# Attention scores on TensorE: three 64-row products in the two row halves instead of two 128-row products, operands split in place, TensorE's order fixed by hand

## The chip, the core and the metric

The kernel runs on one core of a Trainium2 chip. A core has TensorE for matrix products, VectorE, ScalarE and GpSimd for elementwise work, and SyncE, which issues most of the DMA transfers; 16 DMA engines carry them. Each engine works through its own list of instructions in order, and semaphores hold an instruction back until what it needs is there. The metric is the time of the whole kernel on the device in microseconds. Three runs of the kernel before took 747.27, 748.15 and 751.06 us; the median is 748.15.

## What is computed

The reference is attention with a bias that depends on the positions, followed by a two-layer feed-forward part ("MoE" in the names). Four batches, eight heads, 576 positions, head width 64; the feed-forward part has 2304 tokens, 512 inputs and 2048 hidden columns.

```python
scores = scale * np.matmul(q, k.transpose(0, 1, 3, 2))
x = (psi_rel / psi_i)[..., None]
h = np.maximum(x @ w1 + b1, 0.0)
bias = h @ w2
scores = scores + bias.transpose(2, 0, 1)[None, :, :, :]
attn = np.exp(scores - np.max(scores, axis=-1, keepdims=True))
attn = attn / (np.sum(attn, axis=-1, keepdims=True) + 1e-09)
return np.matmul(attn, v).astype(np.float32)
...
h = x @ w_in
g = np.where(pos, h, np.where(neg, 0.0, (h + beta) ** 2 / (4.0 * beta)))
return (g @ w_out).astype(np.float32)
```

All inputs are float32. Products run on TensorE in its rounded form of float32 (fp32r). To keep the accuracy the kernel parts an operand in two: a high part, which is the operand rounded, and a low part, which is what the rounding left out. A product of two operands is then high x high + high x low + low x high.

## The kernel before

The program has three stages, one after the other: the position bias (until 69.84 us in the profile), attention, and the MoE products.

Attention takes the heads in pairs: NP = 4 pairs times B = 4 batches make N = 16 passes n. In a pass the 576 queries of each of the two heads j are cut in four blocks k of 128 rows; the last 64 rows of both heads share a fifth, narrow block "L". A score row has 576 columns and is made in two halves hf of HS = 288, which lie in two banks of PSUM. The pool psS holds two such tiles S, four banks.

**Scores** (`scores`, L441). For each head and half two products of 128 rows add up in PSUM. The first multiplies the queries and, below them in rows 64 to 127, the low part of the queries by the high keys, which lie twice, in rows 0 to 63 and again in rows 64 to 127 (`qs`, `kh`; L455). The second multiplies the queries, with zeros below, by the low keys (`q0`, `kl`; L456). The fifth block has four products per half (L476, L477). VectorE takes S out of PSUM, adds the bias and finds the row's extreme (L458, L478; called the eviction below: tile e, extreme mx); ScalarE makes the exponential in place and sums it (L465, L484).

**Transposes and values.** TensorE transposes e in pieces of 128 x 128 (tiles T, L521; T_L for the narrow block, T_s for what two blocks share). T is parted in hi and lo: ScalarE and VectorE do it (L496, L497), or, for the tiles in POOL, ScalarE copies T to c (L501) and VectorE or GpSimd make hi (L503, L505) and GpSimd lo (L506). The value products O then run over hi and lo in two halves of the queries (L559, L561), ScalarE copies them to x, and R transposes the row sums (L545).

**Preparing a pass** (`prep`, L149). SyncE loads keys and queries in one tile qk (keys in rows 0 to 63, queries in rows 64 to 127, 1216 columns) and the values; GpSimd's queue loads the queries a second time, broadcast into both halves of qa (L167). VectorE casts qk to its high part kh (L163), GpSimd subtracts and gets the low part ls in two pieces (L136). Then two transfers per piece move data between partition halves: the low queries from ls into qa (L199) and the high keys from kh's upper to its lower half (L200). `step` and the table t say in which half step of which earlier pass each of these is issued.

**The order** is made by the program in the order of the calls. A queue holds the transposes and values of earlier blocks; `drain` issues them when the queue is longer than dr[k]. TensorE's instructions are not pinned: the framework's scheduler may move them, and does so.

Beside the passes, attention carries work for the next stage (called guests in the prediction): weights of the first MoE columns (WQ) and its inputs (XQ).

Of the kernel before, what the change touches and what calls it, by code (L numbers as in the profile page):

```python
# [21 lines left out]
P = 128  # L22
# [5 lines left out]
QW = 1216  # L28
# [3 lines left out]
CFG = dict(un=[('paaa', 'paav')[g in (1, 30, 32, 34)] for g in range(NG)], ex=(9, 2, 0, 2, 9), bb=5, mv=1, hi='pvvpv', rb='a', lag=(1, 1), dr=(3, 1, 2, 2, 2), pool=((0, 1), (2, 0), (2, 1), (3, 0), (3, 1)), sb=4, keep=1, drain=2, diag='a', rb2='v', eps='v', rc=2, rbb=1, hb=2, rawb=(2, 2), t=(3, 10, 11, 10, 18, 11, 12, 19), eb=4, seq=0, pb=(6, 9, 12, 14, 16), pq=22, tb=6, ub=12, low0='ppp', anch=(8, 8, 16, 23, 23), low1='ppp', ob=4, gb=4, fin=2, lastp=15, xs=2, sbf=('v', 'v', 'v', 'v', 'v'), bsE=(), ytail='p')  # L32
# [3 lines left out]
FIRST = ((0, 3), (1, 4), (2, 5), (3, 33))  # L36
# [11 lines left out]
def attn_cpb_moe_kernel(ctx, tc, qk, vL, cb, win, wout, lw, ident, ii, out):  # L48
# [26 lines left out]

    qa = [ac.tile([P, 2, QW], F32R, name=f"qa{i}") for i in range(2)]
    last_y, stored, copied, narrow = [], [], {}, []
# [71 lines left out]
    def prep(n):  # L149
# [10 lines left out]
        def high_k():  # L160

            a["k"] = qp.tile([P, QW], F32R, tag="kh", name=f"kh{n}", bufs=CFG["hb"])
            high(nc.vector.tensor_copy(a["k"], a["r"]))  # L163

        def load_q():
            a["q"] = qa[n % 2]
            (keep if n == 1 else pool)(nc.gpsimd.dma_start(out=a["q"][:D], in_=qk[n, D:P].unsqueeze(1).to_broadcast((D, 2, QW))))  # L167

        def load_r():
            a["r"] = lp.tile([P, QW], F32, tag="qk", name=f"qk{n}", bufs=CFG["rawb"][0])  # L170
# [16 lines left out]
        def part(i):  # L187


            def f():  # L190
                if i == 0:
                    a["l"] = qp.tile([P, QW], F32R, tag="kl", name=f"ls{n}")
# [3 lines left out]
                with ExitStack() as after:  # L196
                    if n == 1:
                        after.enter_context(tc.issue_after(stored[-1].ins))
                    nc.sync.dma_start(out=a["q"][D:P, 0, c].bitcast(F32), in_=ls[D:P, c].bitcast(F32))  # L199
                    copied[n] = nc.sync.dma_start(out=kh[D:P, c].bitcast(F32), in_=kh[:D, c].bitcast(F32))  # L200
                if (n, i) == (1, 1):
                    with tc.issue_after(copied[1].ins):
# [7 lines left out]
        return [load_r, load_q, load_v, high_k, high_v, part(0), part(1), v_]  # L210
# [4 lines left out]
    with ExitStack() as ph:  # L215
# [24 lines left out]
        for t in qa:  # L240
            nc.gpsimd.memset(t[D:P, 1, :].bitcast(F32), 0.0)

# [84 lines left out]
        for G in range(NG):  # L327
# [3 lines left out]
            if G == 0:  # L331
                for i in range(3):
                    preps[0][i]()
            for i, g_ in zip((3, 5, 6, 4, 7), CFG["pb"]):
# [22 lines left out]
    def x_tile(z, k, part, name):  # L357
# [4 lines left out]
        if at % 3 == 0 or at == 7:  # L362
            tag, w, n_ = ("qk", QW, CFG["rawb"][0]) if g < 2 else ("v", 10 * D, CFG["rawb"][1])
# [53 lines left out]
    with ExitStack() as ph:  # L417
# [22 lines left out]

        def scores(n, k, qkv, bias):  # L441
            qs, q0, kh, kl = qkv["q"][:, 0], qkv["q"][:, 1], qkv["k"], qkv["l"]
# [5 lines left out]
            if k < 4:  # L448
                e = ep.tile([P, 2 * S], F32, tag="e", name=f"e{n}_{k}")
                for j in range(2):  # L450
                    ps = psS.tile([P, 2, 512], F32, tag="S", name=f"S{n}_{k}_{j}")
                    qc = slice(P * k, P * k + P) if j == 0 else slice(704 + P * k, 704 + P * k + P)
                    for hf in range(2):
# [652 lines left out]
```

## Time and profile before

| | |
|---|---|
| median of three runs | 748.15 us |
| runs | 747.27 to 751.06 us |
| span of the profiled execution | 749.8 us |
| TensorE busy with products | 703.8 us (94%) |
| VectorE, ScalarE, GpSimd busy | 537.5, 518.8, 519.1 us |
| bytes moved by DMA | 103.37 MB |

The profile is of one execution of the kernel; its span runs from the first to the last instruction. It is not one of the three timed runs, and the page states no other time for it. A busy product on TensorE contains the time until its result is out, and the next one starts before that; how densely TensorE works is therefore read from the starts of neighbouring products and not from their durations. A wait is put down to the engine that ended it. DMA share is the mean busy share of the 16 DMA engines.

### The profile page before, as it was taken

To read this page: it belongs to the slowest core of one execution; us is meant where nothing else is said; L and a number is where in the kernel's file an instruction comes from. 1 tells how busy PE (TensorE), PEld (TensorE's weight loads), DVE (VectorE), ACT (ScalarE), POOL (GpSimd) and SP (SyncE) were. 2 spreads that over 40 slices of the span, in tenths; PEclk is the share of its full clock that TensorE was granted. 3 is DMA by queue.
4 is the path that set the end of the run, shared out by engine and by line. 5 is a ranking of instruction groups with operands and counts; after the bars stand their busy time and mean duration, and the time that the engine had idled before them with its cause. 6 is when DMAs were issued, how large, how long until landed. Compare 5 with 4: busy or idle time off the path is not lost.

```text
span 749.8 us, 13722 instructions
## 1 busy us (share of the span) xinstructions
PE 703.8 (94%) x4640; PEld 621.8 (83%) x4640; DVE 537.5 (72%) x1043; ACT 518.8 (69%) x1156; POOL 519.1 (69%) x440
## 2 busy tenths in 40 slices
PE   4687999899999999989999999999999999999997
PEld 1234999888888898989988898989899988888886
DVE  7899888868898888886877776354455465666653
ACT  8896989869888998986656565344444547666563
POOL 9887778858878888871757677565656545665662
PEclk9899999989999999999999999999999999999999
DMA  8887799996997797744364645023021002000002
GB/s 228 231 271 228 200 249 240 238 234 167 233 275 192 186 271 190 177 121 162 95 199 135 197 147 163 35 83 90 7 63 32 1 1 84 1 1 1 0 1 85
DMA packets 58662, 103.37 MB, mean 138 GB/s; under 512 B 12496, under 2 KB 32736, under 8 KB 58592
## 3 DMA queue, kind: packets, MB, share of 16 engines
q1 hardware_dynamic: 56000, 92.31, 43.5%
q0 software_dynamic: 2304, 9.96, 6.4%
q8 instruction: 37, 0.61, 0.3%
q14 instruction: 33, 0.27, 0.1%
q10 hardware_dynamic: 288, 0.22, 0.1%
HBM read 67.38 MB, written 25.12 MB: 123 GB/s over the span
## 4 chain that ended last, share of the span: by engine, by line
PE 64%; DVE 6%; DMA 6%; POOL 5%; ACT 5%; issue 3%; SPq 1%; DVEq 0%; ACTq 0%; POOLq 0%
PE y L716 23%; PE h L716 16%; PE p L716 7%; PE O L559 5%; PE T L521 3%; PE S L455 3%; DMA kh<-kh 2%; PE S L456 2%; POOL lo L506 2%; DVE e L458 2%; PE O L561 1%; DMA v<-in_vL_dram 1%; ACT e L465 1%; POOL ls L136 1%; DMA x<-rT 1%
## 5 line engine op out<-in xcount | busy, mean ns | idle before, releaser
L958 POOL TENSOR_TENSOR gl<-c,gh 128x384 fp32r<-128x384 f32 x64 | 70.8, 1107 | 104.9 <-issue 87.5
L506 POOL TENSOR_TENSOR lo<-c,hi 128x512 fp32r<-128x512 f32 x75 | 101.4, 1368 | 30.2 <-DVE hi L505 27.7
L716 PE MATMUL y<-w1h,gl 128*128 128x512 f32 x288 | 114.0, 396 | 0.0
L716 PE MATMUL y<-w1l,gh 128*128 128x512 f32 x288 | 113.7, 395 | 0.0
L716 PE MATMUL y<-w1h,gh 128*128 128x512 f32 x288 | 112.0, 389 | 0.0
L465 ACT ACTIVATE e<-e,mx 128x576 f32<-128x576 f32 x128 | 100.5, 789 | 15.4 <-DVE mx L458 15.3
L458 DVE CUSTOM_DVE_ANT_0 e<-S,bias 128x576 f32<-128x576 f32 x128 | 94.4, 749 | 18.7 <-PE S L456 18.2
L455 PE MATMUL S<-kh,qa 128*128 128x288 f32 x256 | 80.0, 329 | 10.0 <-DVE mx L458 5.5
L776 ACT ACTIVATE c<-c,half_s 128x384 f32<-128x384 f32 x64 | 39.4, 615 | 60.7 <-DVE c L773 60.7
L456 PE MATMUL S<-ls,qa 128*128 128x288 f32 x256 | 73.6, 305 | 0.0
L521 PE MATMUL T<-id_s,e 128*128 128x128 f32 x512 | 71.6, 276 | 1.3 <-DVE lo L497 0.8
L982 POOL TENSOR_TENSOR gl<-c,gh 128x384 fp32r<-128x384 f32 x32 | 32.7, 1022 | 47.8 <-issue 22.3
L716 PEld LDWEIGHTS y<-w1h,gl 128*128 128x128 f32 x288 | 54.0, 187 | 11.5
L521 PEld LDWEIGHTS T<-id_s,e 128*128 128x128 f32 x512 | 59.4, 143 | 4.1 <-DVE lo L497 1.2
L455 PEld LDWEIGHTS S<-kh,qa 128*128 128x128 f32 x256 | 49.2, 192 | 15.4 <-DVE mx L458 8.8
L284 ACT ACTIVATE u<-lw,nthr 128x576 f16<-128x576 f32 (+17 forms) x104 | 57.8, 647 | 5.5 <-PE B L303 3.0
L716 PEld LDWEIGHTS y<-w1l,gh 128*128 128x128 f32 x288 | 54.0, 187 | 8.0
L716 PEld LDWEIGHTS y<-w1h,gh 128*128 128x128 f32 x288 | 54.1, 188 | 7.7
L303 PEld LDWEIGHTS <-qh 128*32 128x32 f16 x704 | 19.4, 101 | 49.4 <-issue 21.1
L286 POOL TENSOR_SCALAR u<-lw,thr 128x576 f16<-128x576 f32 (+17 forms) x36 | 51.6, 1448 | 5.0 <-PE B L303 3.8
L779 DVE TENSOR_TENSOR c<-h,c 128x384 f32<-128x384 f32 x64 | 35.4, 554 | 26.8 <-ACT c L776 26.0
L954 ACT CAST gh<-c 128x384 fp32r<-128x384 f32 x64 | 32.9, 514 | 30.5 <-DVE c L779 28.6
(266 smaller groups left out, 2112.7 us busy)
## 6 DMA issues: line engine op xcount, KB each, us to landing
bias_d<-y SPq DMA_DIRECT2D x36, 295.5 KB
qk<-in_qk_dram SPq DMA_DIRECT2D x16, 608.0 KB
qa<-in_qk_dram POOLq DMA_DIRECT2D x16, 608.0 KB, 7.2
x<-xT SPq DMA_DIRECT2D x48, 192.0 KB
raw<-in_win_dram SPq DMA_DIRECT2D x16, 512.0 KB
raw<-in_wout_dram SPq DMA_DIRECT2D x16, 512.0 KB
v<-in_vL_dram SPq DMA_DIRECT2D x16, 320.0 KB
qa<-ls SPq DMA_DIRECT2D x32, 152.0 KB
```

Of the source, the lines that this page charges most:

```text
L284: tc.keep_in_program_order(nc.scalar.activation(u[:, :n_], lw1[:, :n_], AF.Sigmoid, bias=nthr[:, m : m + 1], scale=STEEP))
L286: EN[x].tensor_scalar(out=u[:, :n_], in0=lw1[:, :n_], scalar1=thr[:, m : m + 1], scalar2=None, op0=ALU.is_gt)
L455: nc.tensor.matmul(ps[:, hf, :HS], qs[:, qc], kh[:, kc : kc + HS], start=True, stop=False)
L456: nc.tensor.matmul(ps[:, hf, :HS], q0[:, qc], kl[:, kc : kc + HS], start=False, stop=True)
L458: nc.vector.tensor_tensor_reduce(out=ev.rearrange("p (a b) -> p a b", a=2), in0=ps[:, :, :HS], in1=bias[k][:, S * j : S * j + S].rearrange ...
L465: lambda ev=ev, j=j: nc.scalar.activation(ev, ev, AF.Exp, bias=mx[:, j : j + 1], scale=-1.0, accum_out=sm[:, 4 * j + k : 4 * j + k + 1])
L506: r = nc.gpsimd.tensor_tensor(out=lo, in0=m, in1=hi.bitcast(F32), op=ALU.subtract)
L521: nc.tensor.transpose(ps[:, tb, :], e[:, c0 : c0 + P], id_s)
L559: nc.tensor.matmul(ps[:, :w], vs[:, 4 * j + tb, :], src[:, 4 * j + tb, :], start=first and tb == 0, stop=False)
L716: a = nc.tensor.matmul(out, w, x, start=start, stop=stop)
L776: keep(nc.scalar.activation(c, c, AF.Square, scale=0.5, bias=half_s))
L958: keep(nc.gpsimd.tensor_tensor(out=gl, in0=c, in1=gh.bitcast(F32), op=ALU.subtract))
```

## The change

Keys and queries now come in one tile of 128 rows, head 0 in rows 0 to 63 and head 1 in rows 64 to 127, laid out so on the host: first the keys (KW = 640 columns, the last 64 in front once more, so that both heads find the order of columns they need), then the queries (QW = 640: 512, and 128 for the narrow block, in which each head has its 64 and zeros beside them). One cast makes the high part of all of it and two subtractions the low part, in place: qa, its second load, its memsets and the four copies per pass between partition halves are gone.

A score block of both heads is made of 12 products of 64 rows: for each half hf three of them, high x high, low x high and high x low, and of each the one for head 0 in TensorE's rows 0 to 63 (tile position (0, 0)) and the one for head 1 in rows 64 to 127 (position (64, 0)), one behind the other. Both heads' tiles S are open at the same time. The narrow block has six products of 128 rows, which sum both heads' queries over 128 rows with the zeros between.

The queue and `drain` are gone. A table GAPS says what TensorE does behind the scores of each block, and every product and transpose is now kept in the order of the program (`pe_mm`, `pe_tr`).

```diff
-CFG = dict(... ex=(9, 2, 0, 2, 9), ... lag=(1, 1), dr=(3, 1, 2, 2, 2), ... t=(3, 10, 11, 10, 18, 11, 12, 19), ...)
+CFG = dict(... t=(3, 11, 10, 18, 11, 12, 19), ...)
...
-            a["k"] = qp.tile([P, QW], F32R, tag="kh", name=f"kh{n}", bufs=CFG["hb"])
-            high(nc.vector.tensor_copy(a["k"], a["r"]))
-
-        def load_q():
-            a["q"] = qa[n % 2]
-            (keep if n == 1 else pool)(nc.gpsimd.dma_start(out=a["q"][:D], in_=qk[n, D:P].unsqueeze(1).to_broadcast((D, 2, QW))))
+            a["h"] = qp.tile([P, KQ], F32R, tag="kh", name=f"kh{n}", bufs=CFG["hb"])
+            high(nc.vector.tensor_copy(a["h"], a["r"]))
...
-                c = slice(QW // 2 * i, QW // 2 * i + QW // 2)
-                kh, ls = a["k"], a["l"]
-                low(ls[:, c], a["r"][:, c], kh[:, c], L[i])
...
-                    nc.sync.dma_start(out=a["q"][D:P, 0, c].bitcast(F32), in_=ls[D:P, c].bitcast(F32))
-                    copied[n] = nc.sync.dma_start(out=kh[D:P, c].bitcast(F32), in_=kh[:D, c].bitcast(F32))
+                c = slice(KW * i, KW * i + (QW if i else KW))
+                low(a["l"][:, c], a["r"][:, c], a["h"][:, c], L[i])
...
+        def pe_mm(*a, **k):
+            keep(nc.tensor.matmul(*a, **k))
...
         def scores(n, k, qkv, bias):
-            qs, q0, kh, kl = qkv["q"][:, 0], qkv["q"][:, 1], qkv["k"], qkv["l"]
+            kh, kl = qkv["h"][:, :KW], qkv["l"][:, :KW]
+            qh, ql = qkv["h"][:, KW:], qkv["l"][:, KW:]
+            parts_ = ((qh, kh), (ql, kh), (qh, kl))
...
-                for j in range(2):
-                    ps = psS.tile([P, 2, 512], F32, tag="S", name=f"S{n}_{k}_{j}")
...
-                        nc.tensor.matmul(ps[:, hf, :HS], qs[:, qc], kh[:, kc : kc + HS], start=True, stop=False)
-                        nc.tensor.matmul(ps[:, hf, :HS], q0[:, qc], kl[:, kc : kc + HS], start=False, stop=True)
+                pss = [psS.tile([P, 2, 512], F32, tag="S", name=f"S{n}_{k}_{j}") for j in range(2)]
+                for hf in range(2):
+                    for i, (q_, k_) in enumerate(parts_):
+                        for j in range(2):
+                            d = slice(D * j, D * j + D)
+                            kc = D * (1 - j) + HS * hf
+                            pe_mm(
+                                pss[j][:, hf, :HS], q_[d, P * k : P * k + P], k_[d, kc : kc + HS],
+                                start=i == 0, stop=i == 2, tile_position=(D * j, 0),
+                            )
...
+        GAPS = (
+            ((av, 1, 0, 1), (tr, 1, 4)),
+            ((tr, 0, 0), (av, 1, 1, 0)),
+            ((tr, 0, 1), (av, 1, 1, 1)),
+            ((tr, 0, 2),),
+            ((tr, 0, 3), (av, 0, 0, 0)),
+        )
...
+                for f, back, *of in GAPS[k]:
+                    if 0 <= n - back < N:
+                        f(n - back, *of)
+                    for g in later:
+                        g()
+                    later = []
```

In GAPS `tr` is a block's transposes and `av` the value products of one half for one head; the number behind it is how many passes back, and `later` are the exponentials of the block just scored.

Three places show how instructions moved. On TensorE, at the start of pass 8 (S8_k_j is pass 8, block k, head j; kh and ls are the high and low tiles), this stood before:

```order
L455 MATMUL S8_0_0_3512<-kh8_3264,qa0_111 128x288
L456 MATMUL S8_0_0_3512<-ls8_3289,qa0_111 128x288
L455 MATMUL S8_0_0_3512<-kh8_3264,qa0_111 128x288
L456 MATMUL S8_0_0_3512<-ls8_3289,qa0_111 128x288
L455 MATMUL S8_0_1_3518<-kh8_3264,qa0_111 128x288
L456 MATMUL S8_0_1_3518<-ls8_3289,qa0_111 128x288
L455 MATMUL S8_0_1_3518<-kh8_3264,qa0_111 128x288
L456 MATMUL S8_0_1_3518<-ls8_3289,qa0_111 128x288
```

and this stands there now:

```order
L429 MATMUL S8_0_0_3581<-kh8_3327 128x288
L429 MATMUL S8_0_1_3582<-kh8_3327 128x288
L429 MATMUL S8_0_0_3581<-kh8_3327,ls8_3361 128x288
L429 MATMUL S8_0_1_3582<-kh8_3327,ls8_3361 128x288
L429 MATMUL S8_0_0_3581<-ls8_3361,kh8_3327 128x288
L429 MATMUL S8_0_1_3582<-ls8_3361,kh8_3327 128x288
L429 MATMUL S8_0_0_3581<-kh8_3327 128x288
L429 MATMUL S8_0_1_3582<-kh8_3327 128x288
L429 MATMUL S8_0_0_3581<-kh8_3327,ls8_3361 128x288
L429 MATMUL S8_0_1_3582<-kh8_3327,ls8_3361 128x288
L429 MATMUL S8_0_0_3581<-ls8_3361,kh8_3327 128x288
L429 MATMUL S8_0_1_3582<-ls8_3361,kh8_3327 128x288
```

The first head was complete after four of eight products; now the heads alternate and both are complete with the last two of twelve.

At the end of pass 8 TensorE had the transposes of the fourth block (T8_3) behind both heads' first scores of pass 9:

```order
L455 MATMUL S9_0_0_3766<-kh9_3525,qa1_112 128x288
L456 MATMUL S9_0_0_3766<-ls9_3550,qa1_112 128x288
L455 MATMUL S9_0_0_3766<-kh9_3525,qa1_112 128x288
L456 MATMUL S9_0_0_3766<-ls9_3550,qa1_112 128x288
L455 MATMUL S9_0_1_3772<-kh9_3525,qa1_112 128x288
L456 MATMUL S9_0_1_3772<-ls9_3550,qa1_112 128x288
L455 MATMUL S9_0_1_3772<-kh9_3525,qa1_112 128x288
L456 MATMUL S9_0_1_3772<-ls9_3550,qa1_112 128x288
L521 MATMUL T8_3_0_3781<-id_s_145,e8_3_3682 128x128 x4
L521 MATMUL T8_3_1_3790<-id_s_145,e8_3_3682 128x128 x4
```

Now the fourth block's last score products, the third block's transposes, the narrow block and T8_3 follow one another:

```order
L429 MATMUL S8_3_0_3752<-ls8_3361,kh8_3327 128x288
L429 MATMUL S8_3_1_3753<-ls8_3361,kh8_3327 128x288
L432 MATMUL T8_2_0_3770<-id_s_143,e8_2_3691 128x128 x4
L432 MATMUL T8_2_1_3779<-id_s_143,e8_2_3691 128x128 x4
L429 MATMUL S8_L_3793<-kh8_3327 128x288
L429 MATMUL S8_L_3793<-kh8_3327,ls8_3361 128x288
L429 MATMUL S8_L_3793<-ls8_3361,kh8_3327 128x288
L429 MATMUL S8_L_3793<-kh8_3327 128x288
L429 MATMUL S8_L_3793<-kh8_3327,ls8_3361 128x288
L429 MATMUL S8_L_3793<-ls8_3361,kh8_3327 128x288
L432 MATMUL T8_3_0_3803<-id_s_143,e8_3_3751 128x128 x4
```

T8_3 moved ahead of the next pass's scores and of eight or ten value products that stood between.

On VectorE, at the second block of pass 8 (ISA is the eviction and, with mx alone, the read of its extreme), this stood before:

```order
L458 ISA e8_1_3555,mx8_1_3554<-S8_1_0_3556,bias2_1_3051 128x576
L458 ISA mx8_1_3554 128x1
L505 CAST hi7_1_3437<-T7_3_1_3536 128x4x128
L458 ISA e8_1_3555,mx8_1_3554<-S8_1_1_3562,bias2_1_3051 128x576
L458 ISA mx8_1_3554 128x1
L497 TENSOR_TENSOR lo7_1_3438<-T7_L_3571,hi7_1_3437 128x4x64
L497 TENSOR_TENSOR lo7_1_3438<-T7_s1_3580,hi7_1_3437 128x320
```

and now:

```order
L494 TENSOR_TENSOR lo7_1_3501<-T7_L_3613,hi7_1_3500 128x4x64
L494 TENSOR_TENSOR lo7_1_3501<-T7_s1_3622,hi7_1_3500 128x320
L457 ISA e8_1_3634,mx8_1_3633<-S8_1_0_3635,bias2_1_3113 128x576
L457 ISA mx8_1_3633 128x1
L494 TENSOR_TENSOR lo7_1_3501<-T7_L_3613,hi7_1_3500 128x4x64
L457 ISA e8_1_3634,mx8_1_3633<-S8_1_1_3636,bias2_1_3113 128x576
L457 ISA mx8_1_3633 128x1
```

The low parts of pass 7's last transposes moved from behind the second block's evictions to places before and between them.

## Rows read from the trace of the kernel before

**Rows 1.** the page, its first line

```profile
span 749.8 us, 13722 instructions
```

**Rows 2.** windows by stage; columns: PE, PEld, DVE, ACT, POOL busy, clock, DMA

```profile
69.84:340.30 270.46, 255.07 (x1917) 241.57 (x1918) 230.65 (x509) 232.80 (x605) 211.03 (x173) 0.99 0.84 213
340.30:749.80 409.50, 403.07 (x2022) 360.81 (x2020) 245.45 (x407) 225.40 (x445) 245.07 (x213) 1.00 0.23 71
```

**Rows 3.** windows of single passes, S_L to S_L

```profile
127.80:145.00 17.20, 15.93 (x124) 15.39 (x124) 15.71 (x34) 14.88 (x41) 14.44 (x12) 1.00 0.96 250
145.00:166.50 21.50, 18.43 (x118) 17.39 (x118) 13.12 (x31) 14.86 (x39) 13.51 (x12) 0.84 0.90 210
287.50:303.50 16.00, 15.91 (x124) 15.40 (x124) 13.44 (x32) 14.75 (x40) 13.87 (x12) 1.00 0.78 187
```

**Rows 4.** the chain of waits, 120 to 152 us; columns: start, us, what

```profile
134.11 9.52 DMA v<-in_vL_dram
143.69 6.77 DMA kh<-kh
```

**Rows 5.** TensorE's timeline; columns: start, us, instruction, count, idle time before

```profile
78.13 0.38 PE L476 MATMUL S_L<-kh,qa 128*128 128x288 f32 x1
...
290.36 0.64 PE L559 MATMUL O<-lo,vs 128*128 128x256 f32 x4
290.96 0.29 PE L455 MATMUL S<-kh,qa 128*128 128x288 f32 x1
291.09 0.30 PE L456 MATMUL S<-ls,qa 128*128 128x288 f32 x1
...
292.01 1.04 PE L521 MATMUL T<-id_s,e 128*128 128x128 f32 x8
...
293.02 0.29 PE L456 MATMUL S<-ls,qa 128*128 128x288 f32 x1
...
298.86 0.75 PE L559 MATMUL O<-lo,vs 128*128 128x320 f32 x4
...
299.59 0.27 PE L545 MATMUL R<-id_s,sum 128*9 128x128 f32 x1
...
340.27 0.29 PE L476 MATMUL S_L<-kh,qa 128*128 128x288 f32 x1
```

**Rows 6.** TensorE's timeline in the bias stage

```profile
60.81 0.80 PE L303 MATMUL B<-u,qh 128*32 128x512 f16 x8
```

**Rows 7.** weight loads by line; columns: busy us, mean ns of one

```profile
L455 PEld LDWEIGHTS S<-kh,qa 128*128 128x128 f32 x256 | 49.2, 192 | 15.4 <-DVE mx L458 8.8 <-issue 3.4 <-DVE kh L163 1.7
L545 PEld LDWEIGHTS R<-id_s,sum 128*9 128x9 f32 x16 | 1.4, 88 | 0.0
```

**Rows 8.** timeline of the engines, from eviction to transpose

```profile
70.82 0.76 DVE L458 CUSTOM_DVE_ANT_0 e<-S,bias 128x576 f32<-128x576 f32 x1
...
71.51 0.75 DVE L458 CUSTOM_DVE_ANT_0 e<-S,bias 128x576 f32<-128x576 f32 x1
71.62 0.78 ACT L465 ACTIVATE e<-e,mx 128x576 f32<-128x576 f32 x1 [4.34 <-DVE mx L458]
...
72.14 0.30 PE L456 MATMUL S<-ls,qa 128*128 128x288 f32 x1
...
72.48 0.76 DVE L458 CUSTOM_DVE_ANT_0 e<-S,bias 128x576 f32<-128x576 f32 x1 [0.21 <-PE S L456]
...
75.33 0.78 ACT L465 ACTIVATE e<-e,mx 128x576 f32<-128x576 f32 x1
...
76.25 0.20 PEld L521 LDWEIGHTS T<-id_s,e 128*128 128x128 f32 x2 [0.30 <-ACT e L465]
...
244.82 0.37 ACT L496 CAST hi<-T_L 128x256 fp32r<-128x256 f32 x1
...
245.96 0.75 DVE L458 CUSTOM_DVE_ANT_0 e<-S,bias 128x576 f32<-128x576 f32 x1
```

**Rows 9.** the page, costliest groups

```profile
L501 ACT COPY c<-T 128x512 f32<-128x512 f32 x75 | 42.0, 592 | 8.7 <-PE T L521 8.1 <-POOL lo L506 0.6
```

More of the change, by code (lines that the diff above doesn't have):

```diff
@@ L74, in attn_cpb_moe_kernel @@
     ac = loads.enter_context(tc.tile_pool(name="a_const", side="right", bufs=1))
-    qa = [ac.tile([P, 2, QW], F32R, name=f"qa{i}") for i in range(2)]
-    last_y, stored, copied, narrow = [], [], {}, []
+    last_y, stored, narrow = [], [], []
     half_s = wp0.tile([P, 1], F32, name="half_s")
@@ L575, in attn_cpb_moe_kernel @@
                 bias[0][k] = load_bias(0, k)
-        es, eT, sums = {}, {}, {}
-        queue, late = [], []
-        def drain(keep, mid=None, at=0):
-            while len(queue) > keep:
-                at -= 1
-                if at == 0:
-                    mid()
-                for f in queue.pop(0):
-                    f()
+        es, eT, sums, xo = {}, {}, {}, {}
         stores = []
@@ L629, in attn_cpb_moe_kernel, with tr, av @@
         go[0] = True
-        for n in range(N):
+        def tr(n, k):
+            half = k // 2 if k < 4 else 1
+            if k in (0, 2):
+                w = 256 + D * half
+                eT[n, half] = [(tp0, tp1)[half].tile([P, 9, w], F32R, tag=f"{x}{half}", name=f"{x}{n}_{half}") for x in ("hi", "lo")]
+            transposes(n, k, es[n], eT[n, half])
+            if k in (1, 4):
+                shared(n, half, es[n], eT[n, half])
+            if k == 4:
+                nc.vector.reciprocal(out=sums[n], in_=sums[n])
+        def av(n, half, j):
+            values(n, half, j, eT[n, half], qkv[n]["v"])
+            if half and j:
+                recips(n)
+        GAPS = (
[5 more added lines that the diff above has]
+        )
+        for n in range(N + 1):
             p, b = n // B, n % B
@@ L637, in attn_cpb_moe_kernel @@
             for k in range(5):
-                e, later = scores(n, k, qkv[n], bias[p])
-                es[n].append(e)
-                exps = [False]
-                def exp_():
-                    if not exps[0]:
-                        exps[0] = True
-                        for f in later:
-                            exps.append(f())
-                if CFG["ex"][k] == 0:
-                    exp_()
-                step(2 * k)
-                if p + 1 < NP:
-                    for k_ in range(5):
-                        if (b, k) == LB[k_]:
-                            with ExitStack() as after:
-                                if p == 0 and k_ in (0, 1, 4):
-                                    after.enter_context(tc.issue_after(copied[2].ins))
-                                bias.setdefault(p + 1, {})[k_] = load_bias(p + 1, k_)
@@ L671, in inv @@
-                def inv(n=n):
-                    nc.vector.reciprocal(out=sums[n], in_=sums[n])
-                def rc(n=n):
-                    recips(n)
-                if k in (1, 4):
-                    def av(n=n, half=0 if k == 1 else 1):
-                        values(n, half, es[n], eT[n, half], qkv[n]["v"])
-                    queue.append([tr, inv] if k == 4 else [tr])
-                    late.append([CFG["lag"][0 if k == 1 else 1], [av] if k == 1 else [av, rc]])
-                else:
-                    queue.append([tr])
@@ L684, in attn_cpb_moe_kernel @@
-                while late and late[0][0] <= 0:
-                    queue.append(late.pop(0)[1])
-                for x in late:
-                    x[0] -= 1
-                drain(CFG["dr"][k], exp_, CFG["ex"][k])
-                exp_()
-                step(2 * k + 1)
-        queue += [x for _, x in late]
-        while queue:
-            drain(len(queue) - 1)
-            store_x(True)
+                later = []
+                if n < N:
+                    e, later = scores(n, k, qkv[n], bias[p])
+                    es[n].append(e)
+                    step(2 * k)
+                    if p + 1 < NP:
+                        for k_ in range(5):
+                            if (b, k) == LB[k_]:
+                                bias.setdefault(p + 1, {})[k_] = load_bias(p + 1, k_)
```

96 lines of the change are left out of this document (44 added, 52 removed).

## The prediction

> **What bounds the kernel now.** I read the windows by stage first, then single passes of the attention stage, then the chain of waits, then TensorE's timeline. The profiled span is 749.8 us [rows 1]. It lies 1.65 us above the median of the runs (748.15) and inside their range (747.27 to 751.06); the page gives no other time for that execution, so I sum against the span and take 1.65 off at the end. The windows split it in three: position bias until 69.84 us, attention until the last narrow score block at 340, and 409.5 us of MoE, where TensorE is busy 403 us and the change edits nothing [rows 2]. The first stage only loses two memsets and the transfers of two passes; I book zero for both outer stages. Everything is decided in attention, whose window of 270.46 us has TensorE busy 255.07, ScalarE 232.80 and VectorE 230.65, with the 16 DMA engines at 0.84 [rows 2].
>
> One pass handles one batch and head pair; there are 16. From the narrow block S_L of the first pass (78.13) to that of the last (340.27) are 15 passes, 17.48 us each [rows 5]. What TensorE needs in a pass comes from start-to-start times, since its busy time counts pipelined ends twice over: a score product of 288 columns 0.133 us (290.96 to 291.09, eight of them to 292.01), eight transposes 0.88 us (292.01 to one slot before 293.02), so 0.11 each, five value products of 256 columns 0.60 us (290.36 to 290.96), five of 320 columns 0.73 (298.86 to 299.59) [rows 5]. A pass has 40 score products (5.3 us), 40 transposes (4.4), 20 and 20 value products (2.4 and 2.9) and about 0.3 of small ones: **15.3 us**. A pass without guests from the next stage and without DMA trouble takes 16.0 [rows 3], so 0.7 us of waiting. The third and fourth passes take 17.2 and 21.5, with DMA at 0.96 and 0.90 and, in the longer one, a granted clock of 0.84 [rows 3]; the chain there runs through the load of the values (9.52) and the copy kh<-kh (6.77) [rows 4]. These two passes cost 17.2 + 21.5 - 32.0 = 6.7 us over clean ones, 0.45 a pass on the mean. The rest of the 17.48, some 1.0, is guests: weights of the MoE and its inputs, which take ScalarE, VectorE and GpSimd.
>
> **The change, part by part.**
>
> *The copies go.* The second load of the queries, the copies of the low query half and of the high keys into the other partition half, two memsets: by their shapes in the code 64 x 2 x 1216 and four times 64 x 608 words, 1.2 MB less per pass. S of a pass then waits for one load, one cast and one subtraction, all issued a pass or more ahead. I credit the 6.7 us. Below, nothing (the value load stays in that queue, and it is the longer piece of the chain); above, twice as much, if the guests' waits are DMA too.
>
> *The products.* A block of both heads went through 8 products of 128 rows and now through 12 of 64 rows, alternating between the row halves. If two that follow each other stream together, 12 take six slots: 24 pairs and 6 narrow products a pass instead of 40 slots, 10 slots or **1.33 us less TensorE work per pass**, 14.0 instead of 15.3. The trace has no products in row halves. The nearest it has are column quarters in the bias stage: 8 products of 512 columns are done within 0.80 us, the last one's end included, 0.10 each [rows 6], where products that follow one another pay 0.46 ns a column (0.147 for 320, rows 5), 0.24 us each. So the array does run separate tiles at once. For rows I take 0.133 a pair; the bounds are that and 0.266 (one after the other).
>
> A load of weights sits before each product. The load for R, 9 columns, lasts 88 ns and that for S, 128 columns, 192 [rows 7]: 0.10 us of it goes with the columns. One such load hides under a product of 0.133; two in a pair do so only if the halves load side by side. One behind the other they make a pair 0.21. The Trainium skill ("TensorE: Matmul & The Clock Gate", section "LDWEIGHTS (loading the stationary operand)") says that a load's time follows its columns and not its rows, so halving the rows would halve nothing; the rows for R and S agree on columns, and none here shows 64 rows. By that rule with loads in series a block would cost six times twice its 107 ns, 1.28 us, an estimate, against 1.06 now.
>
> Each block of row halves also stands between work on the full array: 8 changes of the tile shape a pass. The trace shows one, between bias and attention, under another wait. From the rows a change costs between nothing and what a product needs beyond its slot until its result is out (0.29 - 0.133, about 0.16 us, rows 5), up to 1.3 us a pass. I take zero, the nearer to how the transposes already alternate with fp32r products without a gap, and keep the other end for a rival. The Trainium skill ("TensorEngine Tiling (Array Packing)", section "Tiling Modes", Key Properties) has a sentence against the change: a change of tiling mode, not just of tile, drains TensorE. It gives no price, and no row here shows it.
>
> *VectorE and GpSimd.* The cast and the two subtractions are over 1280 columns instead of 1216, 5% more, and GpSimd loses a DMA issue per pass: nothing, since both engines have 40 to 60 us of slack in the attention window [rows 2] and these steps run a pass ahead; were they late, 5% of three instructions of a us or two is 0.2 a pass.
>
> *The order.* This is where I expect most of the saving to go. Before, a head's four products are evicted while the other head's run, and T of the fourth row block comes after both heads' first scores of the next pass. Now both heads end together, and T of the fourth block comes right behind S_L. Take E as the end of a block on TensorE. The last product starts at 72.14 and the eviction at 72.48, so 0.21 after E; the second eviction 0.69 later (70.82, 71.51); the exponential 0.80 after its eviction's start (70.82, 71.62); a transpose can load 0.92 after the exponential starts (75.33, 76.25) [rows 8]. T is ready at E + 0.21 + 0.69 + 0.80 + 0.92 = 2.62. Behind the fourth block TensorE has T of the third (0.88) and S_L (0.80), 1.68. It waits at least 0.95, and queued behind it are the value products that are ready and cannot pass. ScalarE has two copies of T out of PSUM, 0.59 each [rows 9], ahead of those exponentials. They can start some 0.2 after the first four transposes (0.44) and end at 1.8; the second exponential then starts at 2.6 and T at 3.5, which makes the wait 1.8. I take 1.3, about the middle. Second place: the second block's eviction on VectorE now stands behind two low parts whose high parts stand behind the first block's exponentials on ScalarE. These end at E + 0.21 + 0.69 + 0.80 + 0.78 = 2.48 (the row of 71.62); from there to the next eviction it takes 1.14 (244.82 to 245.96) [rows 8], so it starts at 3.6, 0.6 late, and the third block, which needs both banks empty, starts up to 0.5 late. The two other gaps hold 2.0 to 2.7 us of TensorE work and just cover the chain; 0.4 for both. Sum of the waits: **2.2 us** where a clean pass has 0.7.
>
> *Sum.* 14.0 + 2.2 = 16.2 for a clean pass (16.0 now). The guests' 1.0 lands partly in waits that are there anyway: 0.5. That is 16.7, against 17.48: 0.78 less in each of 15 passes, 11.7 us. 749.8 - 11.7 - 1.65 = 736.5, say **737 us**.
>
> **The rivals.**
>
> *A, the forecast.* Pairs stream together, the copies' waits are gone, the new order gives half back. 727 to 747 with waits of 1.6 to 2.9 a pass.
>
> *B, the order costs nothing new.* Then 10 slots times 0.133 times 16 (21.3) and 6.7 are gained: 749.8 - 28.0 - 1.65 = 720. For it: TensorE is the busiest engine. Against: ScalarE's 232.80 and VectorE's 230.65 would have to fit into some 242 us in instruction order.
>
> *C, the pair costs more than a product.* Place: every score block. Price: loads in series (0.21 a pair) or about 0.16 at each change of shape; a block then is 0.5 longer. Of the four blocks of a pass about three lie on the chain above, so 18 pairs times (0.21 - 0.133), 1.4 us a pass. It decides from 0.133 + 0.78/18 = 0.18 a pair on; beyond that the kernel is slower than before. At 0.21: 736.5 + 15 x 1.4 = 757.
>
> *D, the change doesn't do what it says:* the halves run one after the other, 0.266 a pair: 18 x 0.133 = 2.4 a pass, 736.5 + 36 = 772. Against it the column quarters.
>
> **How the numbers follow.** A 0.58, B 0.10, C 0.20, D 0.12. Half a percent is 3.7 us, about what a measurement of this kernel can tell from no change: faster means below 744.4, slower above 751.9. Faster: 0.8 of A and B, 0.56. Same: most of what is left of A and a fifth of C, 0.14. Slower: the rest of C, D and a little of A, 0.30. The range leaves out D and half of B: 721 to 762. A alone has 727 to 747.
>
> **What would show it.** In the timeline of TensorE the two heads' products start a few ns apart and pairs 0.13 apart (C: 0.2; D: 0.13 for each product). kh<-kh and qa<-ls are gone from the chain, and DMA falls from 0.84 to about 0.6 in attention. S_L to S_L falls to about 16.7, with TensorE idle before T of the fourth block for 1 to 1.5 us, ended by ScalarE's exponential. MoE keeps its 409.5. I am wrong if that wait is missing (B), or if the score blocks take longer than 1.06 us (C, D).

## The result and the profile after: 756.1 us, 1.1% slower

| | before | after |
|---|---|---|
| median of four runs each, us | 747.88 | 756.14 |
| lowest and highest | 747.27, 751.06 | 754.86, 757.15 |
| ratio of the medians | | 1.0107, 95% interval 1.0085 to 1.0129 |
| span of the profiled execution | 749.8 | 754.6 |

The forecast was 737, with a range of 721 to 762 and a chance of 0.56 for faster. The changed kernel is slower.

The page's first line, and the windows by stage and of three passes, all of the changed kernel (columns as in [rows 2]):

```profile
span 754.6 us, 14003 instructions
...
68.28:342.40 274.12, 253.06 (x2129) 220.20 (x2129) 224.44 (x510) 232.27 (x604) 201.49 (x160) 0.99 0.47 143
342.40:754.60 412.20, 404.90 (x2032) 362.20 (x2031) 246.82 (x406) 225.82 (x446) 245.23 (x213) 1.00 0.23 72
...
131.17:148.76 17.59, 16.09 (x140) 14.12 (x138) 14.79 (x34) 14.85 (x40) 14.11 (x11) 1.00 0.79 251
166.77:184.80 18.03, 16.23 (x137) 14.09 (x137) 15.24 (x34) 15.69 (x41) 13.93 (x11) 1.00 0.36 107
253.86:269.90 16.04, 15.90 (x138) 14.05 (x138) 12.84 (x32) 13.90 (x38) 12.62 (x10) 1.00 0.38 108
```

The attention window is 3.7 us longer than in [rows 2], the MoE window 2.7. DMA fell from 0.84 to 0.47, and the pass of 21.5 us [rows 3] is gone. Yet 15 passes from the first S_L (80.84) to the last (342.40) take 17.44 us each, as good as the 17.48 of before, where 16.7 had been forecast. The cheapest pass is 16.04; the clean one of [rows 3] had 16.00, and the cheapest before, from the S_L at 96.51 to the one at 111.88, 15.37.

TensorE's timeline shows what became of the saved slots (one block of scores with value products around it; x2 means that the two heads' products are grouped in one row):

```profile
256.81 0.76 PE L429 MATMUL O<-lo,vs 128*128 128x256 f32 x5
257.50 0.40 PE L429 MATMUL S<-kh 64*128 64x288 f32 x2
257.74 0.30 PE L429 MATMUL S<-kh,ls 64*128 64x288 f32 x2
257.87 0.29 PE L429 MATMUL S<-ls,kh 64*128 64x288 f32 x2
258.00 0.29 PE L429 MATMUL S<-kh 64*128 64x288 f32 x2
258.14 0.29 PE L429 MATMUL S<-kh,ls 64*128 64x288 f32 x2
258.27 0.29 PE L429 MATMUL S<-ls,kh 64*128 64x288 f32 x2
258.49 0.86 PE L429 MATMUL O<-hi,vs 128*128 128x256 f32 x5
```

The pairs stream as forecast: two products start a few ns apart, most 3 to 4, pairs 0.13. But the first pair needs 0.40 where the others need 0.29, and the next starts 0.24 after it, although it waits for no data; 0.22 lie between the last pair and the first value product, which is again 0.1 late with its result. These are the marks that a product has after a wait, as S_L here behind 0.44 us of idle time:

```profile
253.86 0.40 PE L429 MATMUL S_L<-kh 128*128 128x288 f32 x1 [0.44 <-DVE mx L457]
254.10 0.30 PE L429 MATMUL S_L<-kh,ls 128*128 128x288 f32 x1
```

So TensorE runs empty at each change of tile shape and starts anew. Measured against the slot of the product before, with the late result counted, going into the row halves costs 0.195 us, going back costs 0.143 before a transpose and 0.189 before a value product (the smallest values; the medians are within 7 ns). Two changes for each block, 126 in all (the first two of the 64 blocks follow each other), are about 22 us, **1.4 us a pass**: as much as the 21.3 us of slots that the pairs save.

### The profile page after: what moved, and what is told of

Same layout as the page of the kernel before. It is cut to its first block, busy times and chain, and to the rows that moved or that the text cites. A ratio compares the mean times of both kernels' runs of the same rounds, so it can differ in the third digit from the quotient of the medians.

```text
span 754.6 us, 14003 instructions
## 1 busy us (share of the span) xinstructions
PE 703.7 (93%) x4864; PEld 601.9 (80%) x4864; DVE 532.6 (71%) x1043; ACT 518.3 (69%) x1156; POOL 506.6 (67%) x422
## 4 chain that ended last, share of the span: by engine, by line
PE 57%; DVE 11%; ACT 11%; DMA 4%; issue 4%; POOL 3%; SPq 2%; DVEq 0%; ACTq 0%; POOLq 0%
PE y L692 20%; PE h L692 12%; PE p L692 7%; PE O L429 7%; PE S L429 6%; PE T L432 4%; ACT e L464 4%; DVE e L457 2%; ACT c L498 2%; DVE lo L494 1%; SPq L378 1%; DMA raw<-in_wout_dram 1%; ACT hi L493 1%; DVE x L383 1%; DVE w L116 1%
## 5 line engine op out<-in xcount | busy, mean ns | idle before, releaser
L503 POOL TENSOR_TENSOR lo<-c,hi 128x512 fp32r<-128x512 f32 x75 | 104.7, 1413 | 52.4 <-DVE hi L502 50.0
L457 DVE CUSTOM_DVE_ANT_0 e<-S,bias 128x576 f32<-128x576 f32 x128 | 92.5, 751 | 12.5 <-PE S L429 11.7
L432 PE MATMUL T<-id_s,e 128*128 128x128 f32 x512 | 75.0, 285 | 10.6 <-ACT e L464 8.3
L432 PEld LDWEIGHTS T<-id_s,e 128*128 128x128 f32 x512 | 55.6, 143 | 26.6 <-ACT e L464 20.5
L429 PE MATMUL O<-hi,vs 128*128 128x256 f32 (+1 forms) x320 | 58.3, 312 | 0.7 <-DVE lo L494 0.6
L749 DVE TENSOR_SCALAR c<-h 128x384 f32<-128x384 f32 x64 | 35.3, 552 | 27.0 <-PE h L692 25.2
L429 PE MATMUL O<-lo,vs 128*128 128x256 f32 (+1 forms) x320 | 53.0, 296 | 0.0
```

Of the source, the lines that this page charges most:

```text
L429: keep(nc.tensor.matmul(*a, **k))
L432: keep(nc.tensor.transpose(*a))
L457: nc.vector.tensor_tensor_reduce(out=ev.rearrange("p (a b) -> p a b", a=2), in0=ps[:, :, :HS], in1=bias[k][:, S * j : S * j + S].rearrange ...
L503: r = nc.gpsimd.tensor_tensor(out=lo, in0=m, in1=hi.bitcast(F32), op=ALU.subtract)
L749: keep(nc.vector.tensor_scalar(out=c, in0=h, scalar1=-1.0, scalar2=1.0, op0=ALU.max, op1=ALU.min))
```

## The experiments

Two theories stood against each other. Theory 1: the changes of tile shape eat the gain, and without them the change would win. Theory 2: the order of blocks that is now fixed by hand costs, since passes wait for the chain of eviction, exponential and transpose. Kernels named `six_...`, `one_pair`, `no_copies` and `copies_twice` leave out part of the scores; of them only the time is meant. Each ratio below is against the kernel before, run on the same chip beside it; its median was 746.8 to 747.4 there.

**Six full products** (`six_full`), the changed kernel without row halves:

```diff
-for j in range(2):
-    d, kc = slice(D * j, D * j + D), D * (1 - j) + HS * hf
-    pe_mm(pss[j][:, hf, :HS], q_[d, P * k : P * k + P], k_[d, kc : kc + HS], ..., tile_position=(D * j, 0))
+j = i % 2
+kc = D * (1 - j) + HS * hf
+pe_mm(pss[j][:, hf, :HS], q_[:, P * k : P * k + P], k_[:, kc : kc + HS], start=i < 2, stop=i > 0)
```

> The changed kernel with each score block as six products of 128 rows instead of twelve of 64: as many columns stream (6 x 288), in the same order, with no change of the tile shape. It leaves out part of the scores (both heads' products are mixed). Theory 1 (changes of the tile shape): in the trace of the changed kernel TensorE loses 0.195 us when it goes from the full array to row halves and 0.14 to 0.19 when it goes back, 128 times, 22 us; without them the time falls from 756 to about 736. Theory 2 (the order): TensorE has to wait for the exponentials at the same places anyway, the 22 us turn into longer waits, and the time stays above 750.

Measured: 753.07 us, ratio 1.0072 (1.0050 to 1.0095). Some 22 us less on TensorE bring about 3, and the two intervals overlap a little. Where the rest went stands in the groups by line of TensorE, 70 to 352 us (the last part is the idle time before the group and who ended it); first the changed kernel, then this one:

```profile
L432 PE MATMUL T<-id_s,e 128*128 128x128 f32 x512 | 75.0, 285 | 10.6 <-ACT e L464 8.3 <-ACT x L560 0.4
L429 PE MATMUL O<-hi,vs 128*128 128x256 f32 (+1 forms) x320 | 58.3, 312 | 0.7 <-DVE lo L494 0.6
...
L429 PE MATMUL S_L<-kh 128*128 128x288 f32 x32 | 11.1, 348 | 2.4 <-DVE mx L457 2.4
...
L432 PE MATMUL R<-id_s,sum 128*9 128x128 f32 x16 | 4.4, 274 | 5.9 <-DVE lo L494 5.9
```

```profile
L432 PE MATMUL T<-id_s,e 128*128 128x128 f32 x512 | 72.9, 280 | 14.0 <-ACT e L460 11.9
L429 PE MATMUL O<-hi,vs 128*128 128x256 f32 (+1 forms) x320 | 56.6, 307 | 13.2 <-ACT c L494 11.1 <-DVE lo L490 1.3 <-issue 0.8
```

The waits for ScalarE grew: before transposes from 8.3 to 11.9, before value products from nearly nothing to 11.1. Theory 1 fails as stated: the time does not come near 736.

**The new order on the old products** (`order_only`), the kernel before with `keep` around TensorE's instructions and the table GAPS:

```diff
-nc.tensor.matmul(ps[:, hf, :HS], qs[:, qc], kh[:, kc : kc + HS], start=True, stop=False)
+pe_mm(ps[:, hf, :HS], qs[:, qc], kh[:, kc : kc + HS], start=True, stop=False)
...
-drain(CFG["dr"][k], exp_, CFG["ex"][k])
+for f, back, *of in GAPS[k]: ...
```

> The kernel before, with its products of 128 rows and its copies, but with TensorE pinned to the program's order and the table GAPS of the change. Theory 2 (the order): the pinned order alone costs most of what was lost and hides what was won, 758 to 765. Theory 1 (changes of the tile shape): the order alone is worth little, 745 to 752.

Measured: 758.86, ratio 1.0146 (1.0112 to 1.0181). The table and the fixing together cost 11.4 us. They are not only TensorE's: in the table the exponentials stand behind the first item of a row, where `drain` had put them by `ex`, so ScalarE's order is another one too. The time is the one given for Theory 2. The groups by line:

```profile
L442 PE MATMUL S<-kh,qa 128*128 128x288 f32 x256 | 75.4, 314 | 8.3 <-DMA kh<-kh 6.5 <-DVE t L317 0.9 <-DVE mx L464 0.5
...
L445 PE MATMUL T<-id_s,e 128*128 128x128 f32 x512 | 71.4, 277 | 10.4 <-ACT e L471 9.2 <-DVE lo L503 0.6
```

T waits 9.2 us for the exponential, as in the changed kernel (8.3). But S also waits 6.5 us for the copy kh<-kh, which the changed kernel does not have, so not all of the 11.4 is Theory 2's chain.

**Two entries of the table exchanged** (`swap`): `((tr, 0, 3), (av, 0, 0, 0))` becomes `((av, 0, 0, 0), (tr, 0, 3))`, so that a value product covers the wait of the fourth block's transposes.

> The changed kernel with one line of GAPS turned round: behind the narrow block the value products of the first half come first and the transposes of the fourth block second. The trace of the changed kernel has TensorE idle for 0.82 us before these transposes in 11 of 16 passes. Theory 2 (the order): that wait goes and about 10 to 13 us with it, 743 to 746. Theory 1 (changes of the tile shape): the waits move with the chain from eviction to exponential, and less than 6 us is won, 750 to 756.

Measured: 753.20, ratio 1.0075 (1.0048 to 1.0102); the interval overlaps that of the changed kernel. The time is in the range given for Theory 1 with its moving waits, not in that of Theory 2. The idle time before T fell from 10.6 to 0.4 us, as meant, but the time by about 3: R waits 8.6 us (5.9 in the changed kernel), O 2.6 (0.7), and in 16 blocks the second head's first product starts 0.42 to 0.68 us behind the first head's, most of them 0.47, where its weight load waits for an eviction (the changed kernel has one such late start after its first pass, elsewhere a few ns):

```profile
204.11 0.18 PEld L429 LDWEIGHTS S<-kh 64*128 64x128 f32 x1
204.59 0.18 PEld L429 LDWEIGHTS S<-kh 64*128 64x128 f32 x1 [0.29 <-DVE mx L457]
```

Taking away one wait of this chain moves it.

**No copies**, in two ways. `no_copies` leaves the four copies out in all passes and lets GpSimd clear both planes of qa at the start; `copies_twice` makes them in the first two passes only:

```diff
+if n > 1:
+    return
 with ExitStack() as after:
     ...
     nc.sync.dma_start(out=a["q"][D:P, 0, c].bitcast(F32), in_=ls[D:P, c].bitcast(F32))
```

> The kernel before without its four copies per pass between partition halves; the low part of the queries is left out of the scores. The forecast booked 6.7 us for the waits behind these copies: 741. A rival: the copies hide behind other waits, and less than 2 us goes: 746 to 748.

> The kernel before, with the copies between partition halves made for the first two passes only, so that the start stays as it was; later passes multiply the low query rows that lie there from the second pass, which leaves their low part out. If the copies' waits are real on the path that sets the end: 740 to 743 (6.7 us less). If what they free is lost behind them: 746 to 749.

Measured: 749.01, ratio 1.0017 (0.9994 to 1.0040), and 746.43, ratio 0.9986 (0.9967 to 1.0005). In the first the doubled clearing held the first scores back by 4.8 us, so it decides nothing; the second starts as before (first scores at 69.96, 69.84 before). By it the copies are worth 0.8 us, with an interval from 0.4 us lost to 2.5 won, not 6.7. The second load of the queries stays in this run; no run takes it out by itself. Yet the trace of `copies_twice` has a pass of 16.5 us at the place of the 21.5 in [rows 3], as clean as the forecast had it:

```profile
145.00:161.50 16.50, 15.31 (x118) 14.75 (x118) 13.85 (x33) 15.61 (x41) 13.93 (x12) 1.00 0.62 155
```

The two profiles differ by 6.6 us, the medians by 0.8. The profiled execution of the kernel before was a long one: in the other profiled executions of this study the time lies 1.7 to 1.9 us above the span (2.5 in one), which puts it near 751.6, an estimate, 3.7 above its median; that of `copies_twice` took 744.93, 1.5 below its own.

**The old block order, fixed** (`old_gaps`, `six_old_gaps`, `pin_only`). The table is written so that blocks follow one another as before, once with the twelve halves, once with six full products, once on the kernel before with its products and copies:

```diff
+GAPS = (
+    ((tr, 1, 3),),
+    ((tr, 1, 4), (tr, 0, 0)),
+    ((av, 1, 1, 0), (av, 1, 1, 1), (tr, 0, 1)),
+    ((tr, 0, 2),),
+    ((av, 0, 0, 0), (av, 0, 0, 1)),
+)
```

> The changed kernel with its table written so that TensorE gets the block order of the kernel before (fixed by hand). Theory 2 (the new order's chain is what costs): the pass goes back to what the products allow. The row halves save 1.33 us a pass and the changes of tile shape take about 1.4 back, so the products come out even; the copies' 6.7 us are left as a gain: 739 to 744. Theory 1 (the changes of tile shape by themselves are what costs): the order is no help, 750 to 757.

> As the run before it, but with six products of all 128 rows in place of the twelve of 64 (the two heads' scores are mixed; only the time is meant): no change of tile shape. If with the old order TensorE's own work sets the pass, the 1.33 us a pass that the halves were to save are gained in full: 720 to 728. If the chain eviction, exponential, transpose sets it in this order too, the saved work turns into waits before transposes and the time stays within 4 us of the run before it.

> The kernel before with its own products, copies and block order, TensorE's order fixed by hand, whole blocks one after the other (the scheduler had put single transposes between score products). Theory 2 in its narrow form (which block follows which is what costs): 745 to 750, as before. Rival (fixing by hand is what costs, whatever the order): 755 to 760, as the run with the new order on these products (758.9).

Measured: 760.02 (ratio 1.0166, 1.0141 to 1.0191), 748.09 (1.0002, 0.9987 to 1.0017) and 755.37 (1.0115, 1.0088 to 1.0142). The first two lie outside every range given for them. Two surprises. Fixing whole blocks costs 8 us even in the old order, so Theory 2 in its narrow form, that which block follows which is what counts, fails. The scheduler had put parts of blocks between; that this is what counts fits the rows below, but is not shown alone, because the place of the exponentials changes here as well. The same groups by line, before and then `pin_only`:

```profile
L476 PE MATMUL S_L<-kh,qa 128*128 128x288 f32 x64 | 18.7, 314 | 2.0 <-DVE mx L458 1.4
...
L535 PE MATMUL T_s<-id_s,e 128*128 128x128 f32 x64 | 12.4, 276 | 0.1
```

```profile
L442 PE MATMUL S_L<-kh,qa 128*128 128x288 f32 x64 | 19.3, 324 | 12.4 <-DVE mx L464 12.4
...
L445 PE MATMUL T_s<-id_s,e 128*128 128x128 f32 x64 | 12.9, 283 | 4.1 <-ACT x L569 4.1
```

The narrow block waits 12.4 us for a bank that an eviction empties, with nothing allowed past it; before it was 2.0, some value products or transposes having been placed ahead of it. And in this order the halves cost 12 us over full products, not 3.

**One pair a block** (`one_pair`), to part the change of shape from the pairs: `six_old_gaps` with the last of a block's six products made as a pair of halves. Slots stay the same.

```diff
+if hf and i == 2:
+    for j in range(2):
+        pe_mm(pss[j][:, hf, :HS], q_[d, ...], k_[d, kc : kc + HS], start=False, stop=True, tile_position=(D * j, 0))
+    continue
```

> The kernel of the run with six full products and the old block order (748.1), with the last of each block's six products made as one pair of 64-row products: TensorE's slots stay the same, only a change of tile shape into the halves and one out of them is added per block, 128 in all. (The heads' scores stay mixed in the other five; only the time is meant.) If the changes of shape are what the halves cost: 758 to 761, as the twelve halves in this order (760.0). If it is the streaming of the pairs or their weight loads: 749 to 751, a sixth of the way.

Measured: 756.0, ratio 1.0108 (1.0085 to 1.0130), between the two ranges and nearer the first: 8 of the 12 us come with the changes of shape alone. TensorE's timeline of one block of it:

```profile
256.47 0.29 PE L429 MATMUL S<-kh 128*128 128x288 f32 x1
256.60 0.29 PE L429 MATMUL S<-kh,ls 128*128 128x288 f32 x1
256.82 0.40 PE L429 MATMUL S<-ls,kh 64*128 64x288 f32 x2
257.15 1.09 PE L432 MATMUL T<-id_s,e 128*128 128x128 f32 x8
```

0.22 instead of 0.13 before the pair, and 0.33 before the transposes, although no releaser is named. Of some 22 us of such gaps only 8 reach the time. The groups by line, `six_old_gaps` and then `one_pair`, show why:

```profile
L432 PE MATMUL T<-id_s,e 128*128 128x128 f32 x512 | 70.1, 278 | 5.0 <-DVE lo L490 5.0
...
L429 PE MATMUL S_L<-kh 128*128 128x288 f32 x32 | 11.1, 346 | 11.6 <-DVE mx L453 11.5
```

```profile
L432 PE MATMUL T<-id_s,e 128*128 128x128 f32 x512 | 69.2, 279 | 0.0
...
L429 PE MATMUL S_L<-kh 128*128 128x288 f32 x32 | 11.1, 347 | 9.5 <-DVE mx L462 9.5
```

The wait before T is gone and that before S_L is shorter; all idle time in this stretch fell from 31.0 to 21.6 us, and the gaps stand in its place. The last 4 us between `one_pair` and `old_gaps` I can't assign.

**The scheduler free again** (`half_free`, `six_free`, `free_new`). The first two take queue, `drain` and free scheduling from the kernel before and tiles and products from the changed one (in the first the score products keep their order among themselves, so that pairs stay pairs unless other work is put between); the third is the changed kernel with `keep` taken off, which is the edit shown.

```diff
 def pe_mm(*a, **k):
-    keep(nc.tensor.matmul(*a, **k))
+    nc.tensor.matmul(*a, **k)
```

> The kernel before with its queue, drain and free scheduling, and the new tiles and twelve half-row products (these kept in order, all else left to the scheduler). If fixing the order of whole blocks is what costs, and the products are even by themselves: 744 to 749. If the changes of tile shape cost here too what they cost in the fixed old order (12 us for 128, with two more a pass because the scheduler puts transposes behind the first product): 755 to 762.

> As the run before it, with six products of 128 rows in place of the twelve (the two heads' scores are mixed; only the time is meant) and everything left to the scheduler: ten slots a pass less on TensorE than the kernel before, no change of shape, no copies. If the fixed order is what keeps the saved work from counting: 728 to 738. If the chain eviction, exponential, transpose holds the pass in every order: 742 to 748.

> The changed kernel with nothing fixed on TensorE: the table still gives the program order, the scheduler may move products. It moves the first block of each pass only (its head's products one behind the other, single transposes between). If the fixing as such is what costs: 746 to 750. If the block order of the table costs: 754 to 760.

Measured: 770.14 (ratio 1.0307, 1.0285 to 1.0330), 740.83 (0.9919, 0.9900 to 0.9939) and 764.50 (1.0227, 1.0204 to 1.0249). None lies in a range given for it: `half_free` and `free_new` are worse than either, `six_free` lies between its two. Between `half_free` and `six_free` the waits are in other places. With the scores held in order the scheduler put value products ahead of the third block's scores, where they wait for their low parts. Two rows, `half_free` and then `six_free`:

```profile
L559 PE MATMUL O<-hi,vs 128*128 128x256 f32 (+1 forms) x240 | 43.1, 301 | 16.7 <-DVE lo L497 15.4 <-POOL lo L506 1.3
```

```profile
L552 PE MATMUL O<-hi,vs 128*128 128x256 f32 (+1 forms) x256 | 47.1, 305 | 5.1 <-DVE lo L490 3.3 <-DVE sum L663 1.4
```

Yet all idle time of TensorE from 70 to 352 us is the same, 23.5 and 23.6 us, so waits are not what makes the difference of 29. What `half_free` has more of is changes of shape, 182 and not 126, because in 28 blocks transposes come behind the first product alone:

```profile
193.70 0.39 PE L432 MATMUL S<-kh 64*128 64x288 f32 x1
194.03 0.66 PE L435 MATMUL T<-id_s,e 128*128 128x128 f32 x4
194.61 0.40 PE L432 MATMUL S<-kh 64*128 64x288 f32 x1
```

At the measured 0.195 and 0.143 these 182 come to 31 us, and the 28 lone products take 28 slots more, 3.7 us; both are estimates. So in this order most of the price of the changes reaches the time.

`free_new` shows that the scheduler doesn't mend the new table: it splits pairs in the first block of most passes, running one head's halves behind the other's, and comes out 8 us later than the fixed order. But 4.7 us of it lie before the first S_L of the profile (85.53 us, 80.84 in the changed kernel). TensorE had waited 0.92 us ahead of its first scores and 1.00 ahead of the second block's in both; then the granted clock is at 0.50, the level of 1.2 GHz, for 17.1 us, where the changed kernel has 6.8:

```profile
70.00:87.10 17.10, 16.56 (x68) 13.36 (x68) 8.98 (x22) 9.08 (x21) 2.53 (x3) 0.50 0.68 218
```

All five executions of `free_new` have a mean granted clock of 0.980 to 0.983, those of the changed kernel 0.992 to 0.995. So the 8 us are not a price of the order alone; no run parts the two. The only kernel below the one before by more than the interval is `six_free`, and it leaves work out; I know no way to make both heads' three products in ten slots less on full rows, so no version that does all the work is ahead.

All of it in one table (median us; ratios are above):

| TensorE's order | products and copies of before | twelve halves | six full |
|---|---|---|---|
| scheduler's, program order of before | 747.2 | 770.1 | 740.8 |
| fixed, block order of before | 755.4 | 760.0 | 748.1 |
| fixed, new table | 758.9 | **756.1** | 753.1 |

From the first column to the third TensorE has 21 us less to do, and the copies go; the time falls by some 6, 7 and 6 us. From the third to the second come the changes of shape, 22 us in the two fixed rows and 31 in the first; the time rises by 12, by 3 and by 29. Down a column go the order and, between the first row and the others, the place of the exponentials.

## Why the prediction was wrong

**The step that failed** is the sum "14.0 + 2.2 = 16.2 for a clean pass". It failed in two ways, and the first is its first term. The 14.0 took the change of tile shape as zero; the measured 1.4 a pass makes it 15.4, what a pass had before (15.3). With that one number put in, the sum would have been 737 + 15 x 1.4 = 758, close to 756.1, but that is luck: `six_full`, which has no changes of shape, is at 753.1 and not at 737. The prediction had the event (8 changes a pass), a bound (up to 1.3 a pass; 0.195 is above its 0.16 for one change) and rival C for it, whose 757 is worked out for loads in series, but went for the lower end because transposes alternate with fp32r products without a gap. Those share one tile shape, so that row said nothing on a change of shape. The Trainium skill ("TensorEngine Tiling (Array Packing)", section "Tiling Modes") states that a change of tiling mode drains TensorE; the trace agrees, at 0.143 to 0.195 us each.

**The sum was also of the wrong kind**, and in this order that weighs more. It added TensorE's work and waits as if each were fixed. Of the 19 us between 737 and 756.1 the changes of shape account for about 3 in this order; without them the saved slots turn into waits for ScalarE (`six_full`: 11.9 us before T, 11.1 before O). Only some 0.3 of the saved TensorE time reached the end, in all three orders.

Point by point:

- *Pairs stream together* (A, against D): right, 0.13 a pair.
- *Loads of weights in series* (C's other price): wrong. The halves load side by side, a few ns apart and most of them 182 to 186 ns long. C's other price, about 0.16 at each change of shape, is what came: 0.34 to 0.38 for a block's two.
- *The copies, 6.7 us:* 0.8 by the runs, with an interval that includes no effect. The sum credited a stall that the profiled execution showed and the median hardly holds, and took 1.65 off beside it.
- *The order, 0.7 to 2.2 us of waits a pass:* the mechanism is right. The fourth block's T waits for the exponential; 8.3 us of idle time before T over the 16 passes end so, and 5.9 before R and 2.4 before S_L end with VectorE (the groups of the changed kernel above). The timeline of one such pass in the changed kernel:

```profile
251.63 0.29 PE L429 MATMUL S<-ls,kh 64*128 64x288 f32 x2
...
251.95 0.41 DVE L494 TENSOR_TENSOR lo<-T_s,hi 128x256 fp32r<-128x256 f32 x1
...
252.28 0.85 DVE L174 CAST vs<-v 128x640 fp32r<-128x640 f32 x1
...
253.05 0.74 DVE L457 CUSTOM_DVE_ANT_0 e<-S,bias 128x576 f32<-128x576 f32 x1
...
253.73 0.75 DVE L457 CUSTOM_DVE_ANT_0 e<-S,bias 128x576 f32<-128x576 f32 x1
...
254.03 0.79 ACT L464 ACTIVATE e<-e,mx 128x576 f32<-128x576 f32 x1
...
254.80 0.77 ACT L464 ACTIVATE e<-e,mx 128x576 f32<-128x576 f32 x1
...
255.72 0.42 PEld L432 LDWEIGHTS T<-id_s,e 128*128 128x128 f32 x4 [0.34 <-ACT e L464]
```

  The block's last pair started at 251.63, so it ended near 251.8; the second T could load at 255.72, 3.9 later, where 2.6 to 3.5 had been worked out. The chain itself is that of the forecast: from the first eviction 0.98 to the first exponential (0.80 had been taken), 0.77 to the second, 0.92 to T. What was lacking is in front: VectorE still makes a low part and a cast of the values, so that it evicts 1.3 after the block's end and not 0.21. What it lacked too: fixing whole blocks, with the exponentials in their new place, costs 8 us in the old order and 11.4 in the new one on the old products (6.5 us of waits for copies among them), and the prediction gave it no price.
- *MoE and the start at zero:* MoE is 2.7 us longer (412.20 against 409.50 [rows 2]). What makes MoE longer no run takes apart. The first S_L comes 2.7 us later (80.84 against 78.13 [rows 5]), though the first scores start earlier. Here the granted clock is at 0.50, the level of 1.2 GHz, from 70.50 to 77.30, where before it was at 1.00 throughout (the changed kernel, then before):

```profile
70.50:77.30 6.80, 6.62 (x37) 5.42 (x38) 3.41 (x10) 4.04 (x10) 1.43 (x2) 0.50 0.86 246
```

```profile
69.84:78.13 8.29, 7.57 (x51) 6.36 (x51) 7.05 (x18) 4.91 (x13) 1.30 (x2) 1.00 1.00 265
```

  Before it fell, TensorE had waited 0.92 us ahead of its first scores and 1.00 ahead of the second block's; pairs then start 0.24 apart and not 0.13. Half the clock for 6.8 us costs at most 3.4 us. The fixed order has a part as well: `pin_only`, with the clock at 1.00 there, has its first S_L at 79.80.

## What to carry to other kernels

Before splitting products into row halves, count the changes of tile shape: a block of work between two of them must save more than the pair of changes costs (0.34 to 0.38 us here). Slots saved on the busiest engine are worth little where other engines hold each block by a chain; take the waits as what fills the gap between the engines, not as a term beside the work. Work added to that engine can still cost most of its price, as in `half_free`. And a stall seen in one profiled execution is checked against the spread of the runs before it is credited.

## What the runs showed of the hardware

Two 64-row products of 288 columns, in the two row halves and into different banks, run in the time of one (0.13 us a pair), and their weight loads run side by side. A change between 128-row and 64-row tiles costs 0.195 us into the halves and 0.143 to 0.189 out of them. How much of this shows in the time goes by the order of work: about 3 of 22 us in the new table (`six_full` to the changed kernel), 8 of 22 in the old one (`six_old_gaps` to `one_pair`), where waits shrank in turn, and most of 31 under the scheduler (`six_free` to `half_free`, which differ in the places of their waits too).
